# A Fourier-mixing and gated-MLP kernel: the column transform's rows sorted by parity, with half-width products and a fold that restores the columns

## The chip, the cores and the metric

The kernel runs on one core of one Trainium2 chip. The metric is the device time of one execution in microseconds; the kernel before was run three times (1143.14 to 1143.42 us), and its time is the median, 1143.38 us. The engines are named as in the profile: PE (TensorE matmul), PEld (its weight loads), DVE (VectorE), ACT (ScalarE), POOL (GpSimd) and SP (SyncE, which only issues DMAs).

## The reference

`x` is 2048 rows (S) by 640 columns (D). Two layers, each with a Fourier sublayer and a gated MLP:

```
def _A_ref(x, dft_seq_re, dft_seq_im, dft_hid_re, dft_hid_im):
    a = jnp.einsum("bsd,ed->bse", x, dft_hid_re)
    b = jnp.einsum("bsd,ed->bse", x, dft_hid_im)
    y = jnp.einsum("ts,bse->bte", dft_seq_re, a) - jnp.einsum("ts,bse->bte", dft_seq_im, b)
    return y

def _B_ref(x, w_gate, w_up, w_down):
    g = jnp.einsum("bsd,df->bsf", x, w_gate)
    u = jnp.einsum("bsd,df->bsf", x, w_up)
    h = _sigmoid(g) * u
    return jnp.einsum("bsf,fd->bsd", h, w_down)

for _ in range(2):        # written out twice in the reference
    x = x + _A_ref(_layernorm(x), seq_re, seq_im, hid_re, hid_im)
    x = x + _B_ref(_layernorm(x), w_gate, w_up, w_down)
```

The four DFT matrices hold cosines and sines, so they have mirror symmetry. In the column transform, entry (d, e) is cos or sin of 2 pi d e / 640.

## The kernel before, in words

**Layout.** The rows of `x` stay on chip in one buffer `X` of 16 tiles of 128 rows by 640 columns, four groups q of four tiles. Nearly all else lives in one large buffer, `big`, cut into slots: `take(n, key)` gives n slots of 512 bytes per partition to a name and `drop(key)` frees them, so an instruction that writes a slot waits for the last readers of what stood there. The PSUM banks are `acc`. Operands of matmuls are float16 pairs: `split` (L238) writes a high part on ACT (L241) and the rest as a low part on DVE (L243), and a product has three passes (high-high, high-low, low-high; `PASSES`).

**Fourier sublayer.** `fold_columns` (L621) uses the column symmetry: e holds x[c] + x[640-c] for c = 1 to 320, o holds x[c] - x[640-c]; `fold_double` (L630) puts column 0 in at the end of e. `fold_rows` scales by the layernorm, `fold_join` (L699, lines L707 and L715) combines mirrored row groups and splits into float16. `sequence` (L820, matmuls L846) applies the sequence DFT; its PSUM result goes to `z`, which has the folded column on the partitions (three tiles d of it, 128, 128 and 65 or 64 rows) and the sequence position along the free dimension. `product` (L917, matmul L923) then applies the column DFT: the weight is a 128x128 block of `z`, the moving operand a tile of the folded column matrix `wh`, of which only columns 0 to 320 are used (EC = 321); the other columns follow by mirroring when the result is added. `load_wh` and `split_wh` fetch and split `wh` once, in layer 1; `keep` stores the split form in HBM, and layer 2 loads it from there. One `hidden(q, ph)` step runs the product for the real part (r = 0, nine matmuls) and the imaginary part (r = 1, eight): 17 matmuls of 321 columns. There are eight such steps in each layer, and one `hidden_middle` of nine.

`evict_hidden` (L954) takes the PSUM banks out (for q = 0, ACT L959 and DVE L964 write the difference and sum of the two parts at once; for q > 0 ACT copies, and `combine`, DVE L989, does it later). `join_hidden` (L992, DVE L996) adds or subtracts the results of the two sequence phases `ph`, for row pair `cd` = 0 and 1, into the slot "sum". `add_hidden` (L1001, DVE L1009) adds that to `X` in two instructions: the columns 0 to 320, and the mirrored columns with a reversed read. For the group q = 1 (`SP`) partition 0 of the second row comes from the middle product, and a POOL copy (L1007) puts it in between the two rows' additions.

**Gated MLP.** For each of four blocks b of 512 rows: layernorm, transposes on PE (L569, copied out on ACT and DVE L579; L465 is the DVE instruction that makes the low part before them), then for each of 14 weight tiles j `gate_up` (L1134) and the down product (`down`, L1338). From block 1 of layer 1 on, a form with seven products in place of eight is used (`seven`, L1181), and for it `make_sums` (L1067, POOL, four TENSOR_TENSOR of 128x256, L1072 to L1075, for each weight tile) and `split_sums` prepare sums of weights during block 0 of layer 1. In that block each weight tile is also split (L241, L243) before its first use.

**Tests.** The fast path holds only if the DFT matrices have their symmetry. The kernel checks that on data: POOL issues DMAs of 128x256 tiles of the sequence matrix (L1387), DVE (L1393, L1394, L1396) and ACT (L1371) test them, spread over both layers; `test_hidden_cols` (L1458) does it for the column matrix.

**Order.** The opening (all of layer 1's Fourier sublayer for group 0, and the start of block 0) follows a hand-written list of jobs. After that each job has a due time, counted in PE steps (`at(u, f, ...)`); the jobs of one step are written out in order of due time. Each engine then works through its own instructions in that order, and waits on semaphores for the others. For q = 1 the sequence combine, combine, join, add, join, add of a layer stands in block 0 from `block[0] + 1.6` on, for q = 2 from `block[0] + 14.6`, for q = 3 from `block[1] + 3.5`.

Of the kernel before, what the change touches and what calls it, by code (L numbers as in the profile page):

```python
# [9 lines left out]
F32 = mybir.dt.float32  # L10
# [20 lines left out]
EC = EH + 1  # L31
EPS = 1e-5
# [168 lines left out]
def folded(ctx, tc, pool, dram, big, acc, flag, x, ct, wh, wg, wu, wc, wd, out):  # L201
# [5 lines left out]
    hs = pool.tile([P, 1], F32, name="hs")  # L207
# [110 lines left out]
    def start_identity():  # L318
        nc.vector.tensor_scalar(ident16, ramp, part[:, 34:35], None, op0=OP.is_equal)

        nc.vector.tensor_tensor(hs, ident16[:, 63:64], ident16[:, 64:65], op=OP.add)
        nc.vector.tensor_scalar(hs, hs, -0.5 * CS, CS, op0=OP.mult, op1=OP.add)
        drop("ramp")
        drop("part")
# [296 lines left out]
    def fold_columns(i, k):  # L621

        g = slice(2 * k, 2 * k + 2)
        e, o = (v[:, g] for v in folds(i))
        xg = X[:, 4 * i : 4 * i + 4, :][:, g]
        a, b = xg[:, :, 1 : EH + 1], xg[:, :, D - 1 : EH - 1 : -1]
        nc.vector.tensor_tensor(e[:, :, :EH], a, b, op=OP.add)
        nc.vector.tensor_tensor(o, a, b, op=OP.subtract)

    def fold_double(i, k):  # L630
        g = slice(2 * k, 2 * k + 2)
        e, xg = folds(i)[0][:, g], X[:, 4 * i : 4 * i + 4, :][:, g]
        nc.vector.tensor_scalar(e[:, :, EH:], xg[:, :, 0:1], 2.0, None, op0=OP.mult)
# [258 lines left out]
    def load_wh(r, d):  # L892
        s = take(3, "hr", r, d).f32
        n = P if d < 2 else HALF
        nc.sync.dma_start(s[:n, :EC], wh[r, d * P + 1 : d * P + 1 + n, :EC])
        if r == 0 and d == 2:
            nc.sync.dma_start(s[n : n + 1, :EC], wh[r, 0:1, :EC])
# [5 lines left out]
    def kept_wh(r, d):  # L903

        v = held["h", r, d].f16.rearrange("p (q c) -> p q c", q=2)
        return v[:, 0, :EC] if (r, d) == (1, 2) else v[: KT[r][d], :, :EC]

    def split_wh(r, d, do=ALL):
        v = (held["h", r, d] if ("h", r, d) in held else take(3, "h", r, d)).f16
        n, l = KT[r][d], v[:, 384 : 384 + EC]  # L910
        if (r, d) == (1, 2):
            n, l = HALF, v[HALF:, :EC]
        split(v[:n, :EC], l[:n], held["hr", r, d].f32[:n, :EC], hs[:n] if (r, d) == (0, 2) else CS, do)
# [3 lines left out]
    def product(ps, ph, r, at, m):  # L917
        for d, n in enumerate(KT[r]):
            w = held["h", r, d].f16[:n]
            for zp, wps in PASSES if (r, d) != (1, 2) else ((HI, (HI,)), (LO, (HI,))):  # L920
                z = held["z", ph, d].parts[zp][:n]
                for wp in wps:
                    nc.tensor.matmul(ps[:m, :EC], z[:, at : at + m], w[:, 384 * wp : 384 * wp + EC],  # L923
                                     start=(d == 0 and zp == HI and wp == HI), stop=(d == ND // 2 and zp == LO))
# [26 lines left out]
    def pair_of(s):  # L951
        return s.f32[:, : 2 * EC].rearrange("p (a c) -> p a c", a=2)

    def evict_hidden(q, ph, do=ALL):  # L954

        (a, ka), (b, kb) = held["py", q, ph]
        if q == 0:
            if 0 in do:
                nc.scalar.activation(take(3, "im", ph).f32[:, :EC], b[:, :EC], AF.Copy, scale=CY)  # L959
            if 1 not in do:  # L960
                return
            v, t = pair_of(take(6, "dif", q, ph)), held["im", ph].f32[:, :EC]
            for n, op in enumerate((OP.subtract, OP.add)):
                nc.vector.scalar_tensor_tensor(v[:, n], a[:, :EC], CY, t, op0=OP.mult, op1=op)  # L964
            drop("im", ph)
        else:
            v = pair_of(take(6, "py2", q, ph))
            for n, ps in enumerate((a, b)):
                nc.scalar.activation(v[:, n], ps[:, :EC], AF.Copy, scale=CY)
# [3 lines left out]
    def evict_middle(do=ALL):  # L973
# [5 lines left out]
        if 1 in do:  # L979
            a, ka = held.pop(("py", NB))  # L980
            v = pair_of(held["mid"])[0:1]
            nc.vector.scalar_tensor_tensor(v[:, 0], a[0:1, :EC], CY, v[:, 1], op0=OP.mult, op1=OP.subtract)
            nc.vector.scalar_tensor_tensor(v[:, 1], a[0:1, :EC], CY, v[:, 1], op0=OP.mult, op1=OP.add)
# [8 lines left out]
    def join_hidden(q, cd):  # L992

        u, v = (pair_of(held["dif", q, ph]) for ph in range(2))
        o = pair_of(take(6, "sum", q, cd))
        nc.vector.tensor_tensor(o, u, v, op=OP.subtract if cd else OP.add)  # L996
        if cd:
            drop("dif", q, 0)
            drop("dif", q, 1)

    def add_hidden(q, cd):  # L1001
        r0 = 4 * q + 2 * cd
        s = pair_of(held["sum", q, cd])
        v = s[:, ::-1] if cd else s
        for rows in (slice(0, 1), slice(1, 2)) if q == SP else (slice(0, 2),):
            if q == SP and rows.start:
                nc.gpsimd.tensor_copy(v[0:1], pair_of(held["mid"])[0:1, :: 1 if cd else -1])  # L1007
            for xs, y in ((X[:, r0 : r0 + 2, :EC], v), (X[:, r0 : r0 + 2, D - 1 : EH : -1], v[:, ::-1, 1:EH])):
                nc.vector.tensor_tensor(xs[:, rows], xs[:, rows], y[:, rows], op=OP.add)  # L1009
        drop("sum", q, cd)  # L1010
# [442 lines left out]

    def load_hidden_cols(r, j):
# [3 lines left out]
    def test_hidden_cols(r, j):  # L1458
        a = room(3 * r + j)[: P if j < 2 else EC - 2 * P, :D]
        nc.vector.tensor_reduce(new_max()[: a.shape[0]], a, axis=AX.X, op=OP.max, apply_absolute_value=True)  # L1460
        nc.vector.tensor_tensor(a[:, 1:EH], a[:, 1:EH], a[:, D - 1 : EH : -1], op=OP.subtract if r == 0 else OP.add)
        rest.append(a[:, 1:EH] if r == 0 else a[:, :EC])
        if r == 1 and j == 0:
            square_sum(a[0:1, EC:])

# [450 lines left out]
```

## Time and profile before

| what | value |
|---|---|
| median of three runs (lowest, highest) | 1143.38 us (1143.14, 1143.42) |
| span of the profiled execution | 1142.6 us |
| PE busy | 1107.9 us, 97% |
| DVE busy | 757.1 us, 66% |
| ACT busy | 521.8 us, 46% |
| POOL busy | 372.3 us, 33% |
| `product`'s matmuls (L923) | 290 = 16 hidden steps x 17 + 2 middles x 9 |

The profiled execution has a span of 1142.6 us, 0.8 us below the median of the runs, which also count what lies around the span. "Busy" is the union of the intervals in which an engine works; an engine that is busy 97% of the time on average can still wait for another in a short stretch. In a timeline, a row gives start, duration, engine, line, operation, shapes and count of neighbouring instructions that are shown together, and in brackets the idle time before the first of them and what ended it.

### The profile page before, as it was taken

The numbers are of one execution on the slowest core, as the hardware profiler recorded it, in microseconds if no ns is written. First come the engines' busy times: TensorE is split into PE (matmuls) and PEld (weight loads), VectorE is DVE, ScalarE is ACT, GpSimd is POOL, SyncE is SP. The second block draws the span as 40 slices with busy tenths as digits, with TensorE's granted clock in tenths as the row PEclk, the third lists the DMA queues.
The fourth block names the chain that finished last, engine by engine and source line by source line (L and its number), as shares of the span: only waits on it lengthen the run. The fifth ranks groups of instructions, "written<-read, shape, count | busy, mean of one in ns | idle before, by whom it ended". The sixth has DMA issues, their size and how long they took to land.

```text
span 1142.6 us, 23152 instructions
## 1 busy us (share of the span) xinstructions
PE 1107.9 (97%) x8918; PEld 876.1 (77%) x8918; DVE 757.1 (66%) x1686; ACT 521.8 (46%) x1129; POOL 372.3 (33%) x584
## 2 busy tenths in 40 slices
PE   5599999999999999999999999999999999999997
PEld 2377446788878887888877888778887888788875
DVE  7995888867756777576657767815773568526740
ACT  5975475254524653265524445314551455225420
POOL 2313574432545454422430136021453113221000
PEclk9999999999999999999999999999999999999999
DMA  8427587858495868867412377575658853896401
GB/s 256 145 67 258 199 310 210 256 189 265 153 261 179 263 205 163 276 227 263 155 70 93 106 224 213 133 240 182 210 150 234 285 179 124 159 250 205 149 18 38
DMA packets 156434, 215.94 MB, mean 189 GB/s; under 512 B 74720, under 2 KB 101493, under 8 KB 156314
## 3 DMA queue, kind: packets, MB, share of 16 engines
q1 hardware_dynamic: 137754, 166.44, 48.1%
q0 software_dynamic: 18560, 47.93, 13.8%
q8 instruction: 72, 1.18, 0.4%
q14 instruction: 48, 0.39, 0.1%
HBM read 173.45 MB, written 26.26 MB: 175 GB/s over the span
## 4 chain that ended last, share of the span: by engine, by line
PE 89%; DVE 5%; DMA 2%; ACT 2%; issue 1%; POOL 1%; SPq 0%; DVEq 0%; POOLq 0%; ACTq 0%
PE acc L1181 42%; PE acc L1338 31%; PE acc L1134 10%; PE acc L1274 2%; PE acc L923 2%; PE acc L846 1%; DMA big<-in_ct 1%; DVE big L243 1%; PE twin L355 1%; DMA big<-kept_w 0%; DMA big<-in_wd 0%; DVE big L715 0%; DVE big L673 0%; DVE big L1009 0%; DVE big L707 0%
## 5 line engine op out<-in xcount | busy, mean ns | idle before, releaser
L1181 PE MATMUL acc<-big 128*128 128x256 f16 x4698 | 516.4, 273 | 0.2 <-ACT big L1185 0.2
L1181 PEld LDWEIGHTS <-big 128*128 128x128 f16 x4698 | 459.7, 98 | 54.6 <-issue 0.3
L1338 PE MATMUL acc<-big 128*128 128x320 f16 x2624 | 357.7, 299 | 0.0
L1338 PEld LDWEIGHTS <-big 128*128 128x128 f16 x2624 | 256.8, 98 | 99.5
L1387 POOL DMA_DIRECT2D big<-in_ct x256 | 174.8, 688 | 217.0 <-DVE big L1396 132.8
L1185 ACT ACTIVATE big<-acc 128x256 f32<-128x256 f32 x348 | 128.6, 380 | 237.0 <-PE acc L1181 235.6
L1371 ACT ACTIVATE big<-big 128x768 f32<-128x768 f32 (+8 forms) x104 | 79.6, 765 | 118.4 <-DVE big L1396 83.4
L1249 DVE TENSOR_TENSOR big<-big 128x512 f16<-128x512 f32 x87 | 59.9, 688 | 100.3 <-ACT big L1248 100.0
L1134 PE MATMUL acc<-big 128*128 128x256 f16 (+1 forms) x705 | 114.8, 325 | 1.1 <-DVE big L243 1.1
L1134 PEld LDWEIGHTS <-big 128*128 128x128 f16 x705 | 68.6, 98 | 46.2 <-DVE big L243 1.6
L1353 DVE SCALAR_TENSOR_TENSOR big<-acc,big 128x320 f32<-128x320 f32 x64 | 28.4, 484 | 99.4 <-PE acc L1338 99.3
L1227 ACT ACTIVATE big<-big 128x512 f32<-128x512 f32 x87 | 53.5, 627 | 45.2 <-DVE big L1218 44.6
L243 DVE SCALAR_TENSOR_TENSOR big<-big 128x640 f16<-128x640 f32 (+5 forms) x80 | 64.3, 839 | 9.9 <-ACT big L241 6.8
L241 ACT ACTIVATE big<-big 128x640 f16<-128x640 f32 (+6 forms) x80 | 50.2, 667 | 36.3 <-DMA big<-big 11.0
L1237 DVE SCALAR_TENSOR_TENSOR big<-acc,big 128x256 f32<-128x256 f32 x87 | 36.3, 418 | 40.5 <-PE acc L1181 34.4
L1404 POOL DMA_DIRECT2D big<-in_ct x40 | 27.3, 685 | 109.7 <-ACT big L1185 65.3
L1218 DVE TENSOR_TENSOR big<-big,acc 128x512 f32<-128x512 f32 x87 | 59.1, 679 | 3.6 <-PE acc L1181 3.4
L1248 ACT ACTIVATE big<-big 128x512 f16<-128x512 f32 x87 | 54.5, 626 | 9.6 <-DVE big L1239 8.8
L1217 DVE TENSOR_TENSOR big<-big 128x256 f32<-128x256 f32 x87 | 36.3, 417 | 15.6 <-ACT big L1185 15.5
L521 ACT ACTIVATE big<-big 128x384 f16<-128x384 f32 (+2 forms) x48 | 28.8, 648 | 29.3 <-DVE big L503 15.7
L1394 DVE TENSOR_TENSOR big<-big 128x256 f32<-128x256 f32 x64 | 26.8, 419 | 21.3 <-DMA big<-in_ct 21.2
L923 PE MATMUL acc<-big 128*128 128x321 f16 (+2 forms) x290 | 40.9, 300 | 0.0
(206 smaller groups left out, 1040.9 us busy)
## 6 DMA issues: line engine op xcount, KB each, us to landing
big<-kept_s SPq DMA_DIRECT2D x84, 512.0 KB
big<-kept_w SPq DMA_DIRECT2D x115, 320.0 KB
big<-in_ct POOLq DMA_DIRECT2D x256, 128.0 KB, 4.1
big<-kept_w SPq DMA_DIRECT2D x74, 192.0 KB
kept_w<-big SPq DMA_DIRECT2D x27, 320.0 KB
big<-in_ct POOLq DMA_DIRECT2D x32, 256.0 KB, 5.0
kept_s<-big SPq DMA_DIRECT2D x13, 512.0 KB
big<-in_wg SPq DMA_DIRECT2D x18, 320.0 KB
```

Of the source, the lines that this page charges most:

```text
L243: nc.vector.scalar_tensor_tensor(dl, src, s, dh, op0=OP.mult, op1=OP.subtract)
L923: nc.tensor.matmul(ps[:m, :EC], z[:, at : at + m], w[:, 384 * wp : 384 * wp + EC], start=(d == 0 and zp == HI and wp == HI), stop=(d == ND ...
L1134: nc.tensor.matmul(ps, w[wp][:, d * P : (d + 1) * P], xt[:, xp, :], start=(d == 0 and wp == HI and xp == HI), stop=(d == ND - 1 and wp == LO))
L1181: nc.tensor.matmul(ps, wt, xt, start=start and n == 0, stop=n == len(todo) - 1, skip_group_check=not start)
L1185: nc.scalar.activation(dst, ps, AF.Copy)
L1218: nc.vector.tensor_tensor(v, v, other, op=OP.add)
L1227: nc.scalar.activation(v, v, AF.Sigmoid, scale=SG)
L1248: nc.scalar.activation(s.parts[HI], v, AF.Copy)
L1249: nc.vector.tensor_tensor(s.parts[LO], v, s.parts[HI], op=OP.subtract)
L1338: nc.tensor.matmul(held["pd", e][0][:, :EH], held["ht", j].parts[hp][:, i * P : (i + 1) * P], held["w", 2, j].parts[wp][:, e * EH : (e + 1 ...
L1371: nc.scalar.activation(v, v, AF.Square, accum_out=new_sum()[:p])
L1387: nc.gpsimd.dma_start(v[:, g], bass.AP(ct.tensor, (r * S + row) * S, [[P, NS], [d * S, 16], [1, P]]))
```

## The change

The column transform has a second symmetry: cos(2 pi d (320 - e) / 640) equals cos(2 pi d e / 640) for even d and its negative for odd d, and the sines behave the other way round. So, with the folded columns d sorted into odd ones and even ones, each class needs only the result columns e = 0 to 160 (EW = 161), and the sum and the difference of the two classes give e and 320 - e.

The folded columns are written in parity order: `fold_columns` reads `X` with stride 2 and writes one class after the other. The rows of `wh` are loaded in the same order and only 161 columns wide (eight DMAs in place of seven), and split in eight pieces in place of six, since tile d = 1 holds rows of both classes and is split twice with per-partition scales, into the two halves of a 322-column operand (EQ = 322), with zeros where a row belongs to the other class; `start_identity` computes these scales (six small DVE instructions in place of two). In `product`, tile d = 1 comes first and moves 322 columns into the bank; d = 0 moves 161 into the first half and d = 2 moves 161 into the second half. A hidden step still has 17 matmuls, six of 322 and eleven of 161 columns, and a middle nine, three of 322 and six of 161.

The joined result is then in parity form. A new function `unfold` restores the columns with two TENSOR_TENSOR (128x2x161 and 128x2x160) from the slot "sum" into a new slot "out". For q = 0 they are on DVE, for q = 1 to 3 on POOL. For q = 1, the one-partition copy L1007 becomes a pair of one-partition TENSOR_TENSOR on POOL. `test_hidden_cols` gets one DVE instruction and one ACT square more for each of its six tiles, which test the second symmetry; `turns` makes a column of alternating signs for them.

```
-        a, b = xg[:, :, 1 : EH + 1], xg[:, :, D - 1 : EH - 1 : -1]
-        nc.vector.tensor_tensor(e[:, :, :EH], a, b, op=OP.add)
+        a, b = (v.rearrange("p g (m two) -> p g two m", two=2)[:, :, ::-1]
+                for v in (xg[:, :, 1 : EH + 1], xg[:, :, D - 1 : EH - 1 : -1]))
+        e, o = (v.rearrange("p g (two m) -> p g two m", two=2) for v in (e[:, :, 1:], o))
+        nc.vector.tensor_tensor(e, a, b, op=OP.add)
         nc.vector.tensor_tensor(o, a, b, op=OP.subtract)
...
     def product(ps, ph, r, at, m):
-        for d, n in enumerate(KT[r]):
+        for d, c in ((1, slice(0, EQ)), (0, slice(0, EW)), (2, slice(EW, EQ))):
+            n = KT[r][d]
             w = held["h", r, d].f16[:n]
...
-                    nc.tensor.matmul(ps[:m, :EC], z[:, at : at + m], w[:, 384 * wp : 384 * wp + EC],
-                                     start=(d == 0 and zp == HI and wp == HI), stop=(d == ND // 2 and zp == LO))
+                    nc.tensor.matmul(ps[:m, c], z[:, at : at + m], w[:, 384 * wp : 384 * wp + c.stop - c.start],
+                                     start=(d == 1 and zp == HI and wp == HI), stop=(d == ND // 2 and zp == LO))
...
+    def unfold(s, v, on=nc.vector):
+
+        on.tensor_tensor(s[:, :, :EW], v[:, :, :EW], v[:, :, EW:], op=OP.add)
+        on.tensor_tensor(s[:, ::-1, EH : EW - 1 : -1], v[:, :, : EW - 1], v[:, :, EW : EQ - 1], op=OP.subtract)
...
     def join_hidden(q, cd):
 
         u, v = (pair_of(held["dif", q, ph]) for ph in range(2))
-        o = pair_of(take(6, "sum", q, cd))
+        o = pair_of(take(6, "sum", q, cd, high=2))
         nc.vector.tensor_tensor(o, u, v, op=OP.subtract if cd else OP.add)
...
+        unfold(whole_of(take(6, "out", q, cd)), o, nc.gpsimd if q else nc.vector)
+        drop("sum", q, cd)
...
             if q == SP and rows.start:
-                nc.gpsimd.tensor_copy(v[0:1], pair_of(held["mid"])[0:1, :: 1 if cd else -1])
+                unfold(s[0:1, ::-1], pair_of(held["mid"])[0:1], nc.gpsimd)
```

Three places in the order of the engines. The first is DVE in the opening, where group 0 is joined and added. Before (L996 is the join, L1009 the addition, L443 and L444 the row statistics):

```order
156 L996 TENSOR_TENSOR big_63<-big_63 128x642
157 L1009 TENSOR_TENSOR big_63<-big_63 128x2x321
158 L1009 TENSOR_TENSOR big_63<-big_63 128x2x319
159 L996 TENSOR_TENSOR big_63<-big_63 128x642
160 L443 BN_STATS small1_81<-big_63 128x6 x2
161 L444 BN_AGGR small1_81<-small1_81 128x2
162 L1009 TENSOR_TENSOR big_63<-big_63 128x2x321
```

Now (L1016 is the join, L971 and L972 the unfold, L1031 the addition, L448 and L449 the statistics):

```order
158 L1016 TENSOR_TENSOR big_63<-big_63 128x644
159 L971 TENSOR_TENSOR big_63<-big_63 128x2x161
160 L972 TENSOR_TENSOR big_63<-big_63 128x2x160
161 L1031 TENSOR_TENSOR big_63<-big_63 128x2x321
162 L1031 TENSOR_TENSOR big_63<-big_63 128x2x319
163 L1016 TENSOR_TENSOR big_63<-big_63 128x644
164 L971 TENSOR_TENSOR big_63<-big_63 128x2x161
165 L972 TENSOR_TENSOR big_63<-big_63 128x2x160
166 L448 BN_STATS small1_81<-big_63 128x6 x2
167 L449 BN_AGGR small1_81<-small1_81 128x2
168 L1031 TENSOR_TENSOR big_63<-big_63 128x2x321
```

Two instructions stand between each join and what follows it, the statistics of the first row pair included.

The second place is POOL in block 0 of layer 1, where group q = 1 is joined. Before (L1072 to L1075 are one weight tile's sums, L1007 the copy of the middle row):

```order
55 L1072 TENSOR_TENSOR big_63<-big_63 128x256
56 L1073 TENSOR_TENSOR big_63<-big_63 128x256
57 L1074 TENSOR_TENSOR big_63<-big_63 128x256
58 L1075 TENSOR_TENSOR big_63<-big_63 128x256
59 L1007 COPY big_63<-big_63 1x642
60 L1072 TENSOR_TENSOR big_63<-big_63 128x256
61 L1073 TENSOR_TENSOR big_63<-big_63 128x256
62 L1074 TENSOR_TENSOR big_63<-big_63 128x256
63 L1075 TENSOR_TENSOR big_63<-big_63 128x256
```

Now (L1094 to L1097 are the sums):

```order
55 L971 TENSOR_TENSOR big_63<-big_63 128x2x161
56 L972 TENSOR_TENSOR big_63<-big_63 128x2x160
57 L1094 TENSOR_TENSOR big_63<-big_63 128x256
58 L1095 TENSOR_TENSOR big_63<-big_63 128x256
59 L1096 TENSOR_TENSOR big_63<-big_63 128x256
60 L1097 TENSOR_TENSOR big_63<-big_63 128x256
61 L971 TENSOR_TENSOR big_63<-big_63 1x2x161
62 L972 TENSOR_TENSOR big_63<-big_63 1x2x160
63 L1094 TENSOR_TENSOR big_63<-big_63 128x256
64 L1095 TENSOR_TENSOR big_63<-big_63 128x256
65 L1096 TENSOR_TENSOR big_63<-big_63 128x256
66 L1097 TENSOR_TENSOR big_63<-big_63 128x256
```

An unfold pair stands ahead of the sums whose end the middle row waits for, and the middle row's copy is a pair; the same follows once more, for the second row pair.

The third place is POOL at the end of block 1 of layer 1 (L656 and L663 the last of the fold's scale, L712 and L719 a fill of zeros), where the loads for the tests begin. Before:

```order
126 L416 TENSOR_SCALAR quad0_76<-quad0_76 128x4
127 L656 TENSOR_TENSOR coef0_88<-quad0_76 128x2
128 L712 MEMSET big_63 128x4x63
129 L1387 DMA big_63<-in_ct 128x2x128 x20
130 L403 TENSOR_SCALAR small5_85<-small5_85 128x2
```

Now:

```order
137 L663 TENSOR_TENSOR coef0_88<-quad0_76 128x2
138 L719 MEMSET big_63 128x4x63
139 L971 TENSOR_TENSOR big_63<-big_63 128x2x161
140 L972 TENSOR_TENSOR big_63<-big_63 128x2x160
141 L1409 DMA big_63<-in_ct 128x2x128 x8
142 L971 TENSOR_TENSOR big_63<-big_63 128x2x161
143 L972 TENSOR_TENSOR big_63<-big_63 128x2x160
144 L1409 DMA big_63<-in_ct 128x2x128 x12
```

The unfold pairs of group q = 3 stand ahead of the first eight of these DMAs and between them and the next twelve.

63 lines of the change are left out of this document (43 added, 20 removed).

## The prediction

> **What bounds the kernel now.** I read the page first, then the windows by stage, then the timelines of PE, DVE and POOL where the change acts.
>
> ```profile
> span 1142.6 us, 23152 instructions
> PE 1107.9 (97%) x8918; PEld 876.1 (77%) x8918; DVE 757.1 (66%) x1686; ACT 521.8 (46%) x1129; POOL 372.3 (33%) x584
> ```
>
> PE is busy for all but 35 us, so over the whole span a shorter matmul looks like time. But the share is an average. The windows over the opening and over block 0 of layer 1 say who works in each stretch:
>
> ```profile
> core 0: us, PE busy (x) PEld busy (x) DVE busy (x) ACT busy (x) POOL busy (x), PEclk, DMA share, GB/s
> 40.00:60.00 20.00, 14.67 (x98) 10.94 (x97) 19.27 (x47) 18.30 (x39) 4.42 (x14) 0.91 0.22 57
> 60.00:80.00 20.00, 19.50 (x157) 14.89 (x155) 19.64 (x35) 12.66 (x27) 1.24 (x2) 1.00 0.23 77
> 120.00:140.00 20.00, 20.00 (x94) 9.07 (x93) 15.04 (x22) 7.58 (x13) 12.87 (x13) 1.00 0.61 202
> 140.00:160.00 20.00, 20.00 (x95) 9.04 (x94) 18.52 (x25) 13.32 (x25) 17.49 (x11) 1.00 0.97 368
> ```
>
> In the first two rows DVE is busy for 19.27 and 19.64 of 20 us while PE has room: the opening goes at DVE's pace. In the last two PE is full, with DVE and POOL close behind. The product's matmuls stand, on PE, in these places (the first fence is layer 1, the second layer 2):
>
> ```profile
> 70.42 14.13 PE L923 MATMUL acc<-big 128*128 128x321 f16 x102
> 84.39 1.52 PE L569 MATMUL acc<-ident,big 128*128 128x128 f16 x20
> 85.84 1.39 PE L923 MATMUL acc<-big 128*1 128x321 f16 x9
> ```
>
> ```profile
> 613.56 3.56 PE L846 MATMUL acc<-big 128*128 128x256 f16 x31 [0.29 <-DVE big L715]
> 616.96 14.13 PE L923 MATMUL acc<-big 128*128 128x321 f16 x102
> 631.55 0.73 PE L569 MATMUL acc<-ident,big 128*128 128x128 f16 x10 [0.19 <-DVE big L465]
> 632.45 0.45 PE L569 MATMUL acc<-ident,big 128*128 128x128 f16 x5 [0.16 <-DVE big L465]
> 640.72 1.40 PE L569 MATMUL acc<-ident,big 128*128 128x128 f16 x20
> ```
>
> In both layers six hidden steps (102 matmuls) run into the transposes L569. In layer 2 PE then waits twice for DVE L465, and before that, after the other two hidden steps, for DVE L715. A wait that already ends last grows by what PE saves ahead of it.
>
> **The matmuls.** From 70.42 to 84.39 are 13.97 us, 137 ns each. No 161-column matmul is in the trace. The 128-column transposes take (641.96 - 640.72) / 20 = 62 ns, the next instruction starting at 641.96; on a line between the two, 161 columns take 75 ns. A lower end is 62 ns, an upper one the weight loads' own 98 ns:
>
> ```profile
> L923 PEld LDWEIGHTS <-big x290: 79/98/125, 57.1 to 633.8; 128*128 128x128 f16 x112, 65*128 65x128 f16 x24, 128*1 128x1 f16 x6, 65*1 65x1 f16 x3
> ```
>
> I take 75, since loads at 98 ns overlap in the transposes that start every 62. A hidden step saves 11 x (137 - 75) = 0.68 us, a middle 6 x 62 = 0.37, all 16 and 2 of them 11.6 us (7.3 at 98 ns). [...]
>
> Does any of it reach the end? DVE's rows ahead of the transposes, layer 1 first:
>
> ```profile
> 73.42 0.89 DVE L964 SCALAR_TENSOR_TENSOR big<-acc,big 128x321 f32<-128x321 f32 x2 [0.19 <-ACT big L959]
> 74.35 0.83 DVE L996 TENSOR_TENSOR big<-big 128x642 f32<-128x642 f32 x1
> 83.90 1.50 DVE L465 TENSOR_TENSOR big<-big 128x640 f16<-128x640 f32 x2
> ```
>
> ```profile
> 619.96 0.89 DVE L964 SCALAR_TENSOR_TENSOR big<-acc,big 128x321 f32<-128x321 f32 x2 [1.48 <-ACT big L959]
> 625.48 0.17 DVE L403 TENSOR_SCALAR small<-small 128x2 f32<-128x2 f32 x1 [0.45 <-POOL small L432]
> ```
>
> In layer 1 DVE waited 0.19 us for the hidden steps, then worked on without them until L465, whose two instructions start at 83.90 and about 84.65; PE's transposes start at 84.39 and the second ten need the second. Six steps that end 4.1 us earlier find L465 no earlier: PE waits. **I cost the saving at nothing in layer 1**; its cover is DVE's chain, and only if that were 4 us shorter would the saving appear. In layer 2 it is the same but for one thing: the 1.48 us that DVE waits at 619.96 shrink by 0.68.
>
> **The unfold on DVE.** Two instructions of 322 and 320 elements a pair. A 320-column TENSOR_TENSOR has this price, and reading with stride 2 (L1396 works on every second row of a tile, 128 elements) does not raise it:
>
> ```profile
> L707 DVE TENSOR_TENSOR big<-big 128x320 f32<-128x320 f32 (+1 forms) x32 | 13.6, 483 | 0.0
> L1396 DVE TENSOR_TENSOR big<-big 128x128 f32<-128x128 f32 x128 | 31.7, 290 | 2.2
> ```
>
> 13.6 / 32 = 0.42 us each back to back, so 0.84 a pair and 1.7 for the two that stand ahead of L465. The strided folds I cost at nothing: 290 ns for 128 elements lies on the line through 320 elements at 483 with a fixed part, where a halved rate would not. Against it DVE saves the low parts of `wh`: six of 321 columns (about 0.42 each) become eight of 161 (about 0.27), 0.4 us; and 0.19 us of waiting. Layer 1: +1.1 at the transposes, of which the shorter middle gives back 0.37, and PE and DVE elsewhere perhaps some: I take **+0.5** (0 to 1.1). Layer 2: the first pair is paid by the 0.68, the second eats the 0.45 us ahead of L403 and shifts what follows by about 0.4: **+0.4** (0 to 1.0).
>
> **The unfold on POOL, block 0 of layer 1.** From 109.68 to 177 PE runs without a pause, but the weights are split just ahead of it. POOL's rows, then DVE's, then PE's at one tile:
>
> ```profile
> 117.19 1.32 POOL L1072 TENSOR_TENSOR big<-big 128x256 f32<-128x256 f32 x1 [19.24 <-DVE big L243]
> 118.47 2.91 POOL L1073 TENSOR_TENSOR big<-big 128x256 f32<-128x256 f32 x1
> 122.27 0.72 POOL L1075 TENSOR_TENSOR big<-big 128x256 f32<-128x256 f32 x1
> 122.93 0.71 POOL L1007 COPY big<-big 1x642 f32<-1x642 f32 x1
> 132.66 1.38 POOL L1072 TENSOR_TENSOR big<-big 128x256 f32<-128x256 f32 x1 [1.89 <-DVE big L243]
> 144.79 5.38 POOL L1073 TENSOR_TENSOR big<-big 128x256 f32<-128x256 f32 x1
> ```
>
> ```profile
> 115.30 0.82 DVE L996 TENSOR_TENSOR big<-big 128x642 f32<-128x642 f32 x1
> 123.68 0.89 DVE L1009 TENSOR_TENSOR big<-big 128x321 f32<-128x321 f32 x2 [2.88 <-POOL big L1007]
> 137.40 0.90 DVE L1009 TENSOR_TENSOR big<-big 128x321 f32<-128x321 f32 x2 [2.08 <-POOL big L1007]
> 140.15 1.55 DVE L243 SCALAR_TENSOR_TENSOR big<-big 128x640 f16<-128x640 f32 x2
> 166.32 1.56 DVE L243 SCALAR_TENSOR_TENSOR big<-big 128x640 f16<-128x640 f32 x2 [1.54 <-POOL small L493]
> ```
>
> ```profile
> 141.42 1.03 PE L1134 MATMUL acc<-big 128*128 128x512 f16 x4
> ```
>
> DVE stands still twice (2.88 and 2.08 us) until POOL has done a tile's sums and the middle row. That wait is what the change lengthens: an unfold pair now stands ahead of those sums on POOL, and the middle row becomes a pair. Queued behind the waiting L1009 on DVE are the splits L243 that PE needs.
>
> Price of a pair on POOL: 0.72 us is the fastest row for 256 elements, so 642 elements cost 1.8; at the 1.3 to 2.9 of the rows at 117 and 118, 3.3 to 7.3. I take 2.3, near the fast end, since DVE's work around 116 leaves POOL gaps. The middle pair has 1.8 as its upper end (the same rate) and 0.71, the copy, as its lower; I take 1.4, 0.7 more than now.
>
> First pair: it starts when the join ends, 116.12, and ends at 118.4; the sums would have started at 117.19, so they come 1.2 later, and with 0.7 more for the middle row DVE's L1009 at 123.68 comes 1.9 later. Second: the pair fits into the 1.89 us for which POOL waits before 132.66, but for 0.4, so L1009 at 137.40 comes 1.9 + 0.4 + 0.7 = 3.0 later (1.2 by the low prices, 9 by the high). The first low part of the row at 140.15 ends about 140.97; PE needs it for its third matmul of the tile that starts at 141.42, at 141.85. Of the 3.0 us, 0.88 are slack, and PE waits 2.1. Further on the slack is smaller once: the first L243 at 166.32 ends at 167.14, for a matmul at 167.75, 0.61. So 3.0 - 0.61 = **2.4** in all (0.6 to 8).
>
> The slot "out" also shifts which buffers are reused: in block 0 some of ACT's and SP's instructions now wait for a POOL instruction that they did not wait for before, while POOL is slow (5.38 us at 144.79). I price that between nothing and the 2.9 us of the slower of POOL's rows above, and take **1.0**.
>
> **The test loads behind the unfold.** At the start of the tests POOL issues eight DMAs, and DVE joins q = 3 later; PE's one late wait there is for ACT:
>
> ```profile
> 245.47 5.74 POOL L1387 DMA_DIRECT2D big<-in_ct  x8
> ```
>
> ```profile
> 257.07 0.82 DVE L996 TENSOR_TENSOR big<-big 128x642 f32<-128x642 f32 x1
> 282.29 0.43 DVE L1394 TENSOR_TENSOR big<-big 128x256 f32<-128x256 f32 x1 [1.78 <-DMA big<-in_ct]
> ```
>
> ```profile
> 286.98 6.71 PE L1181 MATMUL acc<-big 128*128 128x256 f16 x60 [0.17 <-ACT big L1185]
> ```
>
> The eight DMAs now stand behind the unfold, which waits for the join: issued from about 260 in place of 245, so the first tests, at 265 on DVE, wait for data 2 to 4 us, and DVE and ACT behind them. PE has some us of slack there except at 286.98, where it has none. I take **+1.0** (0 to 4). The other unfolds (q = 2, and q = 1 to 3 in layer 2) I cost at nothing: PE works in the down products or on weights that need no split there; without that cover each is 1.8.
>
> **The sum.** 1142.6 + 0.8 (the profiled span to the median) + 0.5 + 2.4 + 1.0 + 1.0 + 0.4 = **1148.7 us**.
>
> **Rivals.** *Covered* (within 0.2%, 2.3 us, about what a measurement can tell): POOL's pairs at 1.8 us, the sums' next wait and the slack take it all, the slots and tests cost nothing; 0.6 + 0.5 above now, 1144.5. For it speaks POOL's idle time; against it the two waits on L1007.
>
> *Lock-step* (slower still): POOL's instructions stretch while DVE runs two-input ones (5.38 us at 144.79, with DVE in a row of L243), so the pair costs 4 or more each time: DVE 6 to 9 us late, 1152 to 1157. [...]
>
> *Saving on the path* (faster): the six hidden steps, not DVE, set the transposes. All of it gives 1143.4 - 11.6 = 1131.8; it decides once over 7.6 of the 11.6 us survive the 5.3 lost. The waits of PE in layer 2 speak against it, DVE's 1.48 us wait for it.
>
> **How the numbers follow.** My forecast 0.52, lock-step 0.19, covered 0.13, saving 0.16 (most of it partial, 1135 to 1141). Slower by over 0.2%: 0.71; within: 0.13; faster: 0.16. The range leaves out the saving and the upper tail of lock-step: 1142 to 1155; the forecast's own is 1145.7 to 1151.5.
>
> **What would show it.** L935 (L923 now) near 0.68 us less per hidden step, with PE's waits for L465 longer by as much; DVE's L1031 waiting for POOL in block 0 for 4 to 5 us in place of 2.88 and 2.08; PE idle there by 2 to 5 us; tests waiting for in_ct before 270. Wrong would be: PE's transposes starting 3 us earlier against DVE's chain, POOL pairs that end before DVE asks, or a PE without new pauses before 177.

## The result

The changed kernel takes 1161.78 us (median of four runs, 1160.86 to 1163.79) against 1143.39 us before: a ratio of 1.0162, 95% interval 1.0147 to 1.0176. It is slower by 18.4 us, where the forecast was 5.3 us slower with a range up to 1155. The sign was right, the size was not.

The profile of the changed kernel, first the span and PE's line of its page:

```profile
span 1160.0 us, 23216 instructions
PE 1105.2 (95%) x8918; PEld 874.9 (75%) x8918; DVE 765.5 (66%) x1707; ACT 523.3 (45%) x1143; POOL 394.3 (34%) x614
```

PE's busy time fell by only 2.7 us (1107.9 before) while the span grew by 17.4. Line numbers are new: L935 is the product's matmul (L923), L1031 the addition (L1009), L1016 the join (L996), L245 the low parts (L243), L1156 gate_up (L1134), L1360 the down product (L1338), L1409 the test DMA (L1387), L1415 and L1416 the tests' first instructions (L1393, L1394), L574 the transposes (L569), L1207 the PSUM copy on ACT (L1185).

PE's timeline, the rows of the products and of the new pauses (start, duration, instruction, count, and in brackets PE's idle time ahead of it):

```profile
68.23 9.72 PE L935 MATMUL acc<-big 128*128 128x322 f16 x102
82.60 0.71 PE L574 MATMUL acc<-ident,big 128*128 128x128 f16 x5 [4.65 <-ACT big L468]
...
144.72 37.04 PE L1156 MATMUL acc<-big 128*128 128x512 f16 x163 [2.23 <-DVE big L245]
181.60 44.72 PE L1360 MATMUL acc<-big 128*128 128x320 f16 x328
...
277.60 3.11 PE L1203 MATMUL acc<-big 128*128 128x256 f16 x27 [0.72 <-ACT big L1207]
282.85 11.95 PE L1203 MATMUL acc<-big 128*128 128x256 f16 x108 [2.14 <-ACT big L1207]
298.04 8.38 PE L1203 MATMUL acc<-big 128*128 128x256 f16 x60 [3.24 <-ACT big L1207]
...
616.45 3.35 PE L935 MATMUL acc<-big 128*128 128x322 f16 x34
...
626.29 5.23 PE L853 MATMUL acc<-big 128*128 128x256 f16 x31 [0.29 <-DVE big L722]
...
644.54 0.45 PE L574 MATMUL acc<-ident,big 128*128 128x128 f16 x5 [2.51 <-ACT big L468]
646.79 1.56 PE L574 MATMUL acc<-ident,big 128*128 128x128 f16 x15 [1.80 <-DVE big L470]
...
1101.90 2.45 PE L1203 MATMUL acc<-big 128*128 128x256 f16 x21 [1.14 <-ACT big L1207]
```

The six hidden steps take 9.72 us in place of 14.13, so the matmuls did become as short as planned (95 ns on average). Ahead of the transposes PE now idles 4.65 us in layer 1, and 2.51 and 1.80 in layer 2.

Where did the time come from? The table takes, from PE's timeline of each profile, the start of the rows that end a stage, and gives how much each stage grew against the kernel before. The stages end at the gate_up row at 109.68 of before (opening), the first down product at 177.25 (block 0), the second down product at 302.04 (tests), the first hidden step of layer 2 at 603.73 (rest of layer 1), the next down product at 717.82 (start of layer 2), and the last down product at 1091.30 (end).

| stage | forecast | changed kernel |
|---|---|---|
| opening | +0.5 | +0.26 |
| block 0 of layer 1 | +2.4 and +1.0 for slots | +4.09 |
| tests in layer 1 | +1.0 | +8.38 |
| rest of layer 1 | 0 | 0 |
| start of layer 2 | +0.4 | +3.52 |
| end | 0 | +1.24 |
| span | +5.3 | +17.4 |

The test stage explains 7.4 of the 12 us that the forecast lacked, the start of layer 2 another 3.1, the end 1.2. DVE's and POOL's rows of the test stage answer to those shown of before at 245 and 282:

```profile
262.38 0.82 POOL L971 TENSOR_TENSOR big<-big 128x322 f32<-128x322 f32 x1 [15.17 <-DVE big L1016]
263.27 0.85 POOL L972 TENSOR_TENSOR big<-big 128x320 f32<-128x320 f32 x1
265.19 5.74 POOL L1409 DMA_DIRECT2D big<-in_ct  x8 [1.07 <-issue]
279.40 0.75 POOL L971 TENSOR_TENSOR big<-big 128x322 f32<-128x322 f32 x1 [8.46 <-PE acc L1203]
```

```profile
274.04 0.42 DVE L1415 TENSOR_TENSOR big<-big 128x256 f32<-128x256 f32 x1 [4.13 <-DMA big<-in_ct]
275.52 0.42 DVE L1416 TENSOR_TENSOR big<-big 128x256 f32<-128x256 f32 x1 [1.06 <-DMA big<-in_ct]
...
278.34 0.83 DVE L1016 TENSOR_TENSOR big<-big 128x644 f32<-128x644 f32 x1 [1.27 <-DMA kept_e<-big]
...
290.70 0.43 DVE L1415 TENSOR_TENSOR big<-big 128x256 f32<-128x256 f32 x1 [2.42 <-DMA big<-in_ct]
293.41 0.43 DVE L1416 TENSOR_TENSOR big<-big 128x256 f32<-128x256 f32 x1 [2.28 <-DMA big<-in_ct]
```

The eight DMAs that were issued at 245 now start at 265.19, behind an unfold pair that itself takes 1.7 us but waits 15.17 us for DVE's join. Of the 19.7 us of delay, 4.35 come from the two stages before; the other 15.4 are the 15 that the prediction named. DVE, which works in order, then waits 4.13, 1.06, 2.42 and 2.28 us for the data; behind those tests stand operands that ACT and PE wait for. The PSUM copies L1207 on ACT come late, and PE pauses. Of the stage's 8.38 us, 6.2 are these pauses (6.39 with one of 0.29 us that the rows above leave out, in place of 0.17), and 1.7 are the sixty matmuls behind the last of them, which take 8.38 us and took 6.71 before.

Behind some of the pauses PE also gets less clock. Windows of four microseconds behind four pauses (the column after POOL's is the granted clock, in parts of full speed; the last window begins within the second of two pauses):

```profile
146.00:150.00 4.00, 4.00 (x14) 1.50 (x13) 4.00 (x7) 1.99 (x4) 4.00 (x2) 0.66 1.00 319
298.00:302.00 4.00, 3.96 (x23) 3.01 (x23) 3.29 (x10) 2.44 (x7) 3.67 (x7) 0.61 0.28 99
628.00:632.00 4.00, 4.00 (x30) 3.14 (x29) 2.51 (x4) 2.58 (x5) 0.00 (x0) 0.75 0.02 4
645.00:649.00 4.00, 2.21 (x18) 1.64 (x19) 3.32 (x7) 3.28 (x7) 1.13 (x2) 0.76 0.05 17
```

Block 0 shows the price: after its pause 163 matmuls take 37.04 us, where at the 216 ns of before (67.73 us for 313) they would take 35.3. So a pause of 2.23 us cost about 4.0. Not all of the 1.8 us comes on top, though. In the kernel with q = 3 on DVE, described below, the same pause was not followed by a lower clock, but PE paused a second time for DVE, and block 0 still grew by 3.44 us:

```profile
145.64 13.12 PE L1156 MATMUL acc<-big 128*128 128x512 f16 x60 [2.23 <-DVE big L245]
159.63 22.41 PE L1156 MATMUL acc<-big 128*128 128x512 f16 x103 [0.87 <-DVE big L245]
```

### The profile page after: what moved, and what is told of

The parts are those of the page before. It is cut to its first block, busy times and chain, and to the rows that moved or that the text cites. A ratio compares the mean times of both kernels' runs of the same rounds, so it can differ in the third digit from the quotient of the medians.

```text
span 1160.0 us, 23216 instructions
## 1 busy us (share of the span) xinstructions
PE 1105.2 (95%) x8918; PEld 874.9 (75%) x8918; DVE 765.5 (66%) x1707; ACT 523.3 (45%) x1143; POOL 394.3 (34%) x614
## 3 DMA queue, kind: packets, MB, share of 16 engines
q8 instruction: 72, 1.18, 0.4%
## 4 chain that ended last, share of the span: by engine, by line
PE 83%; DVE 9%; DMA 3%; issue 2%; POOL 1%; ACT 1%; SPq 0%; POOLq 0%; DVEq 0%
PE acc L1203 41%; PE acc L1360 31%; PE acc L1156 8%; DVE big L245 2%; PE acc L1296 2%; PE acc L853 1%; DMA kept_e<-big 1%; DMA big<-in_ct 1%; DVE big L680 1%; DVE big L714 1%; DVE big L722 1%; DMA big<-in_wd 1%; PE acc L574 0%; PE acc L935 0%; DMA big<-in_wg 0%
## 5 line engine op out<-in xcount | busy, mean ns | idle before, releaser
L1360 PE MATMUL acc<-big 128*128 128x320 f16 x2624 | 357.7, 299 | 0.0
L1360 PEld LDWEIGHTS <-big 128*128 128x128 f16 x2624 | 256.7, 98 | 99.5
L1409 POOL DMA_DIRECT2D big<-in_ct x256 | 174.8, 688 | 189.4 <-DVE big L1418 109.9
L1207 ACT ACTIVATE big<-acc 128x256 f32<-128x256 f32 x348 | 127.8, 381 | 239.5 <-PE acc L1203 225.6
L1393 ACT ACTIVATE big<-big 128x768 f32<-128x768 f32 (+10 forms) x110 | 81.6, 742 | 120.0 <-DVE big L1418 81.4
L1156 PE MATMUL acc<-big 128*128 128x256 f16 (+1 forms) x705 | 116.9, 328 | 3.4 <-DVE big L245 3.4
L1156 PEld LDWEIGHTS <-big 128*128 128x128 f16 x705 | 69.1, 99 | 50.0 <-DVE big L245 4.4
L245 DVE SCALAR_TENSOR_TENSOR big<-big 128x640 f16<-128x640 f32 (+5 forms) x78 | 63.2, 848 | 5.1 <-ACT big L243 5.1
L243 ACT ACTIVATE big<-big 128x640 f16<-128x640 f32 (+5 forms) x78 | 48.9, 668 | 30.9 <-issue 12.2
L971 POOL TENSOR_TENSOR big<-big 128x322 f32<-128x322 f32 (+1 forms) x16 | 15.0, 935 | 113.6 <-DVE big L1016 90.3
L1239 DVE TENSOR_TENSOR big<-big 128x256 f32<-128x256 f32 x87 | 36.3, 417 | 16.4 <-ACT big L1207 16.2
L1416 DVE TENSOR_TENSOR big<-big 128x256 f32<-128x256 f32 x64 | 28.0, 438 | 26.8 <-DMA big<-in_ct 26.6
L1415 DVE TENSOR_TENSOR big<-big 128x256 f32<-128x256 f32 x64 | 26.5, 415 | 24.0 <-DMA big<-in_ct 22.8
```

The source lines that it names most:

```text
L243: nc.scalar.activation(dh, src, AF.Copy, scale=s)
L245: nc.vector.scalar_tensor_tensor(dl, src, s, dh, op0=OP.mult, op1=OP.subtract)
L1156: nc.tensor.matmul(ps, w[wp][:, d * P : (d + 1) * P], xt[:, xp, :], start=(d == 0 and wp == HI and xp == HI), stop=(d == ND - 1 and wp == LO))
L1207: nc.scalar.activation(dst, ps, AF.Copy)
L1360: nc.tensor.matmul(held["pd", e][0][:, :EH], held["ht", j].parts[hp][:, i * P : (i + 1) * P], held["w", 2, j].parts[wp][:, e * EH : (e + 1 ...
L1393: nc.scalar.activation(v, v, AF.Square, accum_out=new_sum()[:p])
```

## The experiments

The runs of one changed kernel lie 0.1 to 1.4% apart (in the widest case 1162 to 1178 us), so the medians settle only the large steps, and the small ones are read from the stages of the profiles. A profile is one execution; with q = 3 on DVE, q = 1 on DVE, no unfold (both versions) and all wide it is the fastest one of its kernel. This table holds, for each kernel, the growth of each stage against the kernel before, as above.

| kernel | median us | opening | block 0 | tests | start of layer 2 | end | span |
|---|---|---|---|---|---|---|---|
| changed | 1161.8 | +0.26 | +4.09 | +8.38 | +3.52 | +1.24 | +17.4 |
| q = 3 on DVE | 1155.2 | +1.18 | +3.44 | +1.55 | +1.66 | +1.23 | +9.1 |
| loads first | 1157.2 | +0.33 | +4.09 | +2.67 | +2.01 | +1.22 | +10.4 |
| q = 1 on DVE | 1164.4 | +0.35 | +4.13 | +8.67 | +3.51 | +1.23 | +17.7 |
| no unfold | 1147.6 | -1.20 | 0.00 | -0.33 | +2.57 | +1.24 | +2.3 |
| no unfold, layer 2 wide | 1144.6 | -1.71 | -0.01 | -0.33 | +0.02 | +1.23 | -0.7 |
| all wide | 1163.5 | -0.37 | +4.10 | +5.93 | +1.76 | +1.23 | +12.5 |
| layer 2 wide | 1161.5 | +0.40 | +4.10 | +8.26 | +3.04 | +1.23 | +16.9 |
| no new test | 1159.0 | +0.06 | +4.08 | +8.23 | +3.31 | +0.05 | +15.6 |

**The test loads: unfold of q = 3 on DVE.**

```
-        unfold(whole_of(take(6, "out", q, cd)), o, nc.gpsimd if q else nc.vector)
+        unfold(whole_of(take(6, "out", q, cd)), o, nc.gpsimd if 0 < q < 3 else nc.vector)
```

> The changed kernel (1161.8 us) with the unfold of group q = 3 on DVE in place of POOL, so that POOL's test loads no longer stand behind it. Theory (the test loads came 20 us late, DVE's tests waited for them, and PE lost 6.2 us of pauses and about 2 us of lowered clock between 226 and 306): most of that stage's 8.4 us go, 1153.5 to 1156. Rival (the pauses come from the new reuse of slots, which stays as it is, as at the join that waits for the store kept_e): 1159 or more.

Measured: 1155.22 us (1153.81 to 1162.74), ratio 1.0126 (1.0091 to 1.0160). The test stage fell from +8.38 to +1.55. POOL and DVE there:

```profile
247.43 5.76 POOL L1409 DMA_DIRECT2D big<-in_ct  x8
```

```profile
270.10 0.42 DVE L1415 TENSOR_TENSOR big<-big 128x256 f32<-128x256 f32 x1
...
274.02 0.83 DVE L1016 TENSOR_TENSOR big<-big 128x644 f32<-128x644 f32 x1 [2.04 <-DMA kept_e<-big]
...
288.52 0.42 DVE L1416 TENSOR_TENSOR big<-big 128x256 f32<-128x256 f32 x1 [1.80 <-DMA big<-in_ct]
```

The loads are back at 247, and the first test waits for nothing. The slots are the same as in the changed kernel, and the wait for the store kept_e is still there, so reuse of slots can hold no more than the 1.55 us that are left.

**The same, with the unfold left on POOL: loads first.**

```
-                at(u, load, *key)
+                at(u - 1.9 if first and u < block[1] + 8 else u, load, *key)
```

> The changed kernel, with the unfold of q = 3 still on POOL, but the first eight test DMAs of layer 1 put ahead of it in POOL's order (two loads are due 1.9 steps earlier). The next twelve still stand behind the second unfold. Theory (it is the loads' place behind an unfold that waits for DVE's join, not POOL's time, that cost the stage): of the 8.4 us between the first down products and block 2, at least 4 go. Rival (POOL's work or its contention with DVE costs the time): less than 2 go.

Measured: 1157.16 us (1153.43 to 1161.39), ratio 1.0128 (1.0095 to 1.0160). The stage fell to +2.67, by 5.7 us, though POOL still does all of the unfold (four of the eight loads are now issued at 237.20, before those of the kernel before, and four at 247.23). Two instructions of 0.8 us were not the main cost: that was their place in an in-order queue, where they wait for DVE, with DMAs behind them that wait for nothing. The second pair still stands ahead of the next twelve loads; the stage is 1.1 us longer than with all of the unfold on DVE.

**Block 0: unfold of q = 1 on DVE.**

```
-        unfold(whole_of(take(6, "out", q, cd)), o, nc.gpsimd if q else nc.vector)
+        unfold(whole_of(take(6, "out", q, cd)), o, nc.gpsimd if q > 1 else nc.vector)
```

> The changed kernel with the unfold of group q = 1 on DVE in place of POOL. Theory (in block 0 of layer 1 the unfold on POOL holds up the middle row, and so DVE's splits): the pause of 2.23 us near 144.7 and the 1.8 us of lowered clock behind it go, 1157 to 1159. Rival (DVE itself is the bound there, and its own four instructions of about 0.5 us put the splits off as far): 1161 to 1163.

Measured: 1164.38 us (1162.32 to 1178.48), ratio 1.0225 (1.0161 to 1.0289). The rival holds: block 0 costs +4.13, as with POOL (the median lies 1.4 us above the rival's range, among runs 16 us apart). DVE's rows in the changed kernel and in this one:

```profile
125.50 0.89 DVE L1031 TENSOR_TENSOR big<-big 128x321 f32<-128x321 f32 x2 [2.82 <-POOL big L972]
...
141.10 0.90 DVE L1031 TENSOR_TENSOR big<-big 128x321 f32<-128x321 f32 x2 [2.83 <-POOL big L972]
...
142.51 0.82 DVE L245 SCALAR_TENSOR_TENSOR big<-big 128x640 f16<-128x640 f32 x1
```

```profile
130.69 0.91 DVE L971 TENSOR_TENSOR big<-big 128x322 f32<-128x322 f32 x1
131.63 0.90 DVE L972 TENSOR_TENSOR big<-big 128x320 f32<-128x320 f32 x1
...
141.23 0.89 DVE L1031 TENSOR_TENSOR big<-big 128x321 f32<-128x321 f32 x2 [2.82 <-POOL big L972]
```

The second addition starts at 141.10 with POOL and at 141.23 with DVE. DVE's pair takes 1.8 us there in place of about 1.0 while POOL works beside it, its splits come later, and POOL's sums wait for those splits. The first of POOL's sums ahead of that addition starts within 0.14 us in both kernels, and both times it is DVE that releases it (changed kernel, then q = 1 on DVE):

```profile
135.61 1.38 POOL L1094 TENSOR_TENSOR big<-big 128x256 f32<-128x256 f32 x1 [0.36 <-DVE big L245]
```

```profile
135.75 1.38 POOL L1094 TENSOR_TENSOR big<-big 128x256 f32<-128x256 f32 x1 [3.57 <-DVE big L245]
```

In this stretch DVE and POOL pass work to each other, and work added to either one delays both.

**Is the saving on the path? No unfold at all.** The joined form is added as it stands (the columns are not restored), and the middle row is copied as before.

```
-        o = pair_of(take(6, "sum", q, cd, high=2))
+        o = pair_of(take(6, "sum", q, cd))
...
-        unfold(whole_of(take(6, "out", q, cd)), o, nc.gpsimd if q else nc.vector)
-        drop("sum", q, cd)
...
-        s = whole_of(held["out", q, cd])
+        s = whole_of(held["sum", q, cd])
...
-                unfold(s[0:1, ::-1], pair_of(held["mid"])[0:1], nc.gpsimd)
+                nc.gpsimd.tensor_copy(v[0:1], whole_of(held["mid"])[0:1, :: 1 if cd else -1])
```

> The changed kernel without any unfold: the joined parity form is added to X as it stands, so the columns are not restored, and the middle row is copied as before. It keeps the shorter matmuls. Theory (the saved matmul time becomes waiting of PE, since DVE sets the end of both layers' Fourier stretches): 1142 to 1147, at most 1.5 us better than before. Rival (the saving is on the path and only the unfold hides it): 1132 to 1136.

Measured: 1147.57 us (1146.92 to 1148.09), ratio 1.0037 (1.0023 to 1.0051): slower than before, with nothing of the unfold in it. Block 0 and the tests cost nothing, so both of these stages were the unfold's. The opening gains 1.20 us, but the shorter matmuls are not its source: DVE is ahead there in all the changed kernels, as the account of the prediction below shows. And the start of layer 2 loses 2.57 us although less is computed there. The median lies 0.6 us above the theory's range, and the loss in layer 2 asked for the next run.

**The same with layer 2's product widened** (tiles d = 0 and d = 2 move their 161 columns twice, another product):

```
+                    wide = d != 1 and folding[0]
+                    mv = w[:, 384 * wp : 384 * wp + c.stop - c.start]
-                    nc.tensor.matmul(ps[:m, c], z[:, at : at + m], w[:, 384 * wp : 384 * wp + c.stop - c.start],
+                    nc.tensor.matmul(ps[:m, slice(0, EQ) if wide else c], z[:, at : at + m], twice(mv) if wide else mv,
```

> The kernel without any unfold again (columns not restored), with the product of layer 2 alone widened: tiles d = 0 and d = 2 move their 161 columns twice, into both halves of the bank (another product). Layer 1 keeps the narrow matmuls. Without the widening this kernel lost 2.6 us in layer 2's Fourier stretch against the kernel before. Theory (the narrow matmuls only make PE wait there, and the clock falls behind the pauses): with 5.8 us more of matmul work that stage costs no more, 0 to 2.6 us against before, and fewer pauses. Rival (the matmuls are on the path): the stage gets 4 to 6 us longer.

Measured: 1144.58 us (1143.77 to 1145.92), ratio 1.0013 (1.0003 to 1.0023). With 5.8 us of matmul work put back, the start of layer 2 is shorter by 2.55 us, at +0.02 against before. PE's rows at this place, without and with the widening:

```profile
612.03 5.22 PE L853 MATMUL acc<-big 128*128 128x256 f16 x31 [0.29 <-DVE big L722]
617.10 9.73 PE L935 MATMUL acc<-big 128*128 128x322 f16 x102
628.71 0.45 PE L574 MATMUL acc<-ident,big 128*128 128x128 f16 x5 [1.88 <-ACT big L468]
630.95 1.78 PE L574 MATMUL acc<-ident,big 128*128 128x128 f16 x15 [1.79 <-DVE big L470]
```

```profile
611.51 3.56 PE L853 MATMUL acc<-big 128*128 128x256 f16 x31 [0.28 <-DVE big L722]
...
630.41 0.45 PE L574 MATMUL acc<-ident,big 128*128 128x128 f16 x5 [0.16 <-DVE big L470]
```

The same 31 sequence matmuls take 5.22 us where PE had paused three times ahead of them (0.89, 0.47 and 0.29 us), and 3.56 where only the last of these pauses was left. The windows over them show the granted clock at 0.57 without the widening and at 1.00 with it:

```profile
612.00:616.00 4.00, 3.97 (x21) 2.85 (x22) 2.10 (x4) 1.81 (x4) 0.00 (x0) 0.57 0.50 164
```

```profile
611.00:615.00 4.00, 3.72 (x35) 3.12 (x33) 3.22 (x6) 2.94 (x5) 0.00 (x0) 1.00 0.50 168
```

These matmuls stand on the path, since ACT waits for their sums and DVE for ACT: in the changed kernel, where they take 5.23 us, ACT waits 1.24, 0.54, 0.68 and 0.62 us for them, and DVE 0.74, 0.45, 0.59 and 0.52 us for ACT; before, where they take 3.56, there is one such wait each, 1.24 and 0.75 us. So the shorter matmuls made room for pauses, behind the pauses the clock was lower, and the lower clock stretched work that does count. All five runs without the widening are slower than all ten with it. That the pauses bring the lower clock is not shown for every case: two kernels with the same three pauses kept 3.56 us (the last section).

**The unfolds with wide products: all of them, and layer 2's alone.** All else as in the changed kernel; the edit is the one above, with `wide = d != 1` for all of them.

> The changed kernel with every matmul of the product 322 columns wide: the tiles d = 0 and d = 2 move their 161 columns twice, into both halves of the bank, so the product is another one. All else is as in the changed kernel. Theory (the narrow matmuls' saving is worth next to nothing, and PE's pauses that take its place lower the clock): 1159 to 1164, within 2.5 us of the changed kernel. Rival (the narrow matmuls save on the path what their widths say, 11.6 us): 1171 to 1174.

Measured: 1163.53 us (1156.98 to 1172.28), ratio 1.0202 (1.0157 to 1.0247); the profiled run has a span of 1155.1 us, less than the changed kernel's 1160.0. 11.6 us more of matmul work cost nothing that shows in runs this far apart; the slowest of the four, 1172.28 us, lies in the rival's range, but the profile's opening and start of layer 2, where the matmuls are, are both shorter than the changed kernel's.

> The changed kernel, unfolds included, with the product of layer 2 widened in the same way (another product). Layer 2's Fourier stretch costs 3.5 us against before in the changed kernel. Theory: 1.5 to 2.5 with the wide matmuls, the price of the two unfold pairs on DVE, since the pauses and the lowered clock behind them go. Rival: 3.5 + 5.8 = 9.3.

Measured: 1161.52 us (1159.70 to 1169.38), ratio 1.0176 (1.0136 to 1.0216). The start of layer 2 is +3.04, above the 1.5 to 2.5 of the theory and far from the rival's 9.3. The kernel with all products wide has +1.76 there, with the same matmuls, the same pause of 1.72 us, and this difference behind it (layer 2 wide, then all wide):

```profile
648.00:652.00 4.00, 4.00 (x24) 2.56 (x23) 1.28 (x3) 1.10 (x4) 2.13 (x8) 0.64 0.46 128
```

```profile
645.00:649.00 4.00, 4.00 (x38) 3.38 (x36) 1.39 (x3) 1.00 (x3) 2.22 (x9) 1.00 0.41 142
```

The clock fell to 0.64 in one and stayed at 1.00 in the other; 24 matmuls against 38 in four microseconds. So the unfold's own price at the start of layer 2 is about 1.76 us, and what comes on top here is the clock. The kernel with q = 3 on DVE, where the 31 matmuls kept their 3.56 us, has +1.66 with narrow matmuls.

**The end: no new test.** The second symmetry's test is left out.

```
-        b = room(3 * r + j)[: P if j < 2 else EC - 2 * P, D : D + EW - 1]
-        nc.vector.scalar_tensor_tensor(b, a[:, : EW - 1], turns()[: b.shape[0]], a[:, EH : EW - 1 : -1], op0=OP.mult,
-                                       op1=OP.subtract if r == 0 else OP.add)
-        square_sum(b)
```

> The changed kernel without the new test of the second symmetry (the DVE instruction and the ACT square that test_hidden_cols gained are left out, and turns with them). Theory (they stand ahead of a PSUM copy L1207 on ACT in the last block, for which PE waits 1.14 us at 1101.9): that pause goes, and nothing else changes, 1.2 us off the span behind the last block's products. Rival (the pause comes from the changed slots): it stays.

Measured: 1159.03 us (1156.05 to 1160.98), ratio 1.0130 (1.0110 to 1.0150). The stage fell from +1.24 to +0.05, and the pause of 1.14 us is gone. On ACT, in the changed kernel, the new square (128x160) and one that was there before stand ahead of the copy L1207 for which PE waits:

```profile
1099.77 0.34 ACT L1393 ACTIVATE big<-big 128x160 f32<-128x160 f32 x1 [1.05 <-DVE big L1492]
...
1101.03 0.47 ACT L1393 ACTIVATE big<-big 1x319 f32<-1x319 f32 x1 [0.82 <-DVE big L1496]
...
1101.50 0.36 ACT L1207 ACTIVATE big<-acc 128x256 f32<-128x256 f32 x1
```

None of these versions beats the kernel before. With the unfold left out and layer 2's product kept wide, the profiled span is 0.7 us below before, and 1.9 below if the new test's 1.24 us are taken off too; but that profile is the fastest of ten runs, and their median is 1.5 us above that of the thirteen runs of before. The idea has little to win in this schedule, since the matmuls that it shortens were not what the stretch waited for.

## Why the prediction was right and wrong

- *The matmuls' saving costed at nothing*: right. Six hidden steps shortened to 9.72 us and PE idled 4.65 us at layer 1's transposes. With all products wide and the unfold in place the opening is 0.37 us shorter than before, with narrow ones 0.26 longer, so in these profiles nothing of the saving came through.
- *The matmul's price*: right. 17 matmuls in a step came to 95 ns on average (9.72 / 102); the estimate from 137 and 75 ns gives 97.
- *The unfold on DVE, opening* (+0.5): measured +0.26, within its bounds, but by luck: three sizes were off and nearly cancel. DVE reached the eviction ahead of the join 2.46 us earlier than before (70.96 against 73.42) where the sum had 0.6; over half of that arose at about 25, where DVE's wait for ACT's split shrank from 1.65 to 0.34 us. The two pairs took 2.0 us in place of 1.7. So L470 (L465 before) started 0.64 us earlier (83.26 against 83.90), where 1.1 later was forecast. PE lost that again, since its clock was low behind the 4.65 us:

```profile
84.00:88.00 4.00, 3.92 (x30) 3.01 (x31) 3.86 (x11) 3.04 (x6) 2.76 (x5) 0.59 0.31 83
```

  In the same four microseconds of before, and with all products wide, it was 1.00; the middle's nine matmuls took 1.39 and 1.40 us there, and 1.70 in the changed kernel.
- *Block 0* (2.4 and 1.0 for slots): the result of the chain came near the forecast, its inside only in part. The two additions on DVE, corrected for the 0.26 us of the opening, were 1.6 and 3.4 us later where 1.9 and 3.0 were said, and PE paused 2.23 us where 2.1 to 2.4 were said. But DVE's waits for POOL, which were to grow to 4 to 5 us, were 2.82 and 2.83. The pairs on POOL took 3.5 and 2.6 us and not 2.3, the first tile's sums behind them less than before, and DVE itself came later: its addition at 120.74 took 1.94 us beside POOL's sums (0.88 before, beside a sum that took 2.91), and four splits at 132.53 took 3.87 beside POOL's second unfold pair (2.75 before, when POOL stood still for 1.89 us of it). No run shows the 1.0 us for slots. What stood in its place was 1.8 us of lowered clock behind the pause, or, where the clock stayed, the second pause of 0.87 us. The sum (3.4 against 4.09) was near, for one wrong reason.
- *The test loads behind the unfold* (+1.0, bounds 0 to 4): **this is the step that failed**. The mechanism was as described, down to the 15 us that the loads wait behind the unfold; its price was 8.38 us. I took the slack of "some us" from PE's side for one late test and did not add up the waits: four instructions of the tests waited, 9.9 us in all (1.78 before), each in DVE's in-order queue ahead of what ACT and PE wait for. PE's pauses came to 6.2 us more than before, and 1.7 us of slower matmuls followed. The second unfold pair stands ahead of the next twelve loads too, which the sum did not have; by the kernel with the loads first, which keeps it, that is worth about 1 us (+2.67 against +1.55).
- *The clock* (no term): the sum had every matmul at the speed of before. Lowered clock behind pauses is in the measured time of the opening (0.59 over four microseconds), block 0 (0.66), the tests (0.61) and the start of layer 2 (0.75 and 0.76).
- *Start of layer 2* (+0.4, bounds 0 to 1.0): wrong. The DVE pairs cost about 1.8 (wide products, no lowered clock), and the lowered clock behind the pauses brought it to 3.5. A pair takes more than the 0.84 us that the prediction gave it; DVE's rows in the changed kernel:

```profile
635.41 0.50 DVE L971 TENSOR_TENSOR big<-big 128x322 f32<-128x322 f32 x1
635.94 0.49 DVE L972 TENSOR_TENSOR big<-big 128x320 f32<-128x320 f32 x1
636.46 1.56 DVE L1031 TENSOR_TENSOR big<-big 128x642 f32<-128x642 f32 x2
```

  They start 0.53 us apart, each when the one ahead has ended, 1.05 for the pair. Why L972 waits for L971, whose result it does not read, the trace does not show.
- *The end* (nothing): an omission. The new test's instructions were counted in the change but had no term in the sum; they cost 1.24.
- *The rivals*: "saving on the path" was refuted by both wide runs, "covered" by block 0. "Lock-step" (1152 to 1157) came nearest to the time measured, but from block 0, where DVE was 3.4 us late and not 6 to 9. Of the stretching that it supposed something is there, on DVE's side: with q = 1 on DVE, its second unfold pair in block 0 takes 0.91 and 0.90 us with POOL at work, and the pair in the rows above, with POOL idle, 0.50 and 0.49. What stretches them no run shows.

## What to carry to other kernels

When an instruction is put into an in-order queue, price it by what it waits for and by what stands behind it, not by its own length: 1.7 us of POOL work, waiting 15 us ahead of loads that waited for nothing, made most of a loss of 8.4 us, and 5.7 of it went when loads were put first. Before shortening PE's work, look which engine ends the stretch: PE time that turns into pauses can come back as a loss, because the clock can be lower behind them: in the kernel without the unfold it was 0.57 where it was 1.00 with layer 2's product wide, and the same 31 matmuls took 5.22 us in place of 3.56. Add up every late instruction in a chain against one slack, and give each new instruction a line in the sum, however small.

## What the runs showed of the hardware

The granted clock can be lower behind pauses that are short. Behind a pause of 2.23 us it was 0.66 over four microseconds, and behind a pause of 1.72 us, with short transposes on both sides, 0.64. The same pauses do not always do it. Behind the 2.23 us of the kernel with q = 3 on DVE it was 1.00:

```profile
146.00:150.00 4.00, 4.00 (x21) 1.80 (x19) 4.00 (x7) 2.91 (x5) 3.27 (x2) 1.00 0.99 331
```

The 1.72 us cost 1.3 us in one kernel and nothing in another, and the 31 matmuls behind three pauses of 0.89, 0.47 and 0.29 us took 5.23 us in the changed kernel and, with q = 3 on DVE, these:

```profile
619.72 3.56 PE L853 MATMUL acc<-big 128*128 128x256 f16 x31 [0.28 <-DVE big L722]
```

So equal pauses stand here with and without the loss, and what decides between them no run shows. The spread between runs of the changed kernels (up to 1.4%, where the thirteen runs of before lie within 0.2%) stays open too: in the widest case, q = 1 on DVE, the slowest run, 1178.48 us, had a mean granted clock of 0.985 and the fastest, 1162.32 us, 0.986.
